# Three edits at the start of a gated attention and MLP kernel: z in rows of four tokens, one accumulator copy on VectorE, scores from the fifth value pair

## The chip, the cores and the metric

The kernel runs on one core of one Trainium2 chip. Its engines are TensorE (PE; PEld is its weight load), VectorE (DVE), ScalarE (ACT), GpSimd (POOL) and SyncE (SP), each with a queue of its own that runs in order. The metric is device time in microseconds (us) of one execution, as the median of several runs.

## The reference

```python
scores = (1/S) * z @ z.T            # per batch: S = 3008 tokens, 64 features
attn   = maximum(scores, 0) ** 2    # S x S
x      = u * (attn @ v)             # S x 256
h      = x @ w_in                   # 256 -> 2048
out    = (h * cos(h)) @ w_out       # 2048 -> 256
```

There are 8 batches; inputs and output are float32. `attn` is symmetric, since both sides of the score are z. The kernel computes in 16-bit floats with 32-bit accumulators.

## The kernel before, in words

The tokens of a batch are cut into 24 rows (k) of 128 and 6 columns (J) of 512. A slot s is one column of one batch; batch 0 has slots 0 to 5. For a slot, `phase_a` or `phase_a_first` multiplies the squared scores of the column with v for all 24 rows, which gives the attention output, transposed, in two halves dh of 128 features. `phase_b` then runs the two matrix products of the hidden layer for earlier slots. No scheduler moves anything: `manual_schedule` keeps each engine's instructions in the order in which the Python code issues them.

**Scores.** `emit_score` makes one score group: two matmuls on half of the array each (L194) into one of the two-bank tiles E, a ReLU by ScalarE into r (L204), and a square by VectorE into a piece A (L209 or L212). A group holds two of the four rows of a block I against column J (h = 0 or 1). Groups come in a fixed order: batch, column J, block I, h. Pieces under the diagonal are later turned by DMA transposes on SP's queue rather than computed.

**Values.** `emit_value` issues the matmuls with v (L258). A row k gives a pair for each dh: the upper 64 tokens go to one accumulator bank, the lower 64 to another, and the two run side by side on the two halves of the array. So a half dh has two banks to add up: one dh uses the two M banks, the other the two banks of an E tile. A step is one such pair.

**The first columns.** Slots 0, 1 and 2 go through `phase_a_first`, in which scores of the next column are made between the steps. With `run` = 2 (slots 1 and 2), steps 0 to 7 are rows 0 to 7 of dh 0, 8 to 15 the same rows of dh 1, 16 to 23 rows 8 to 15 of dh 0, and so on up to step 45; step 46 is the last half row for both. `lo, hi` and `n` say behind which steps the n scores stand (12, 12 and 14 in the three slots): score i stands behind step `lo + (hi - lo) * i // (n - 1)`. In slots 1 and 2 the two gate multiplications of the slot before (`gate_mul`, L286) are issued at step 15, ahead of a score at that step. Score groups that a slot makes itself are needed by it from step 16 on: the first two groups hold rows 8 to 11, the next two rows 12 to 15.

**The end of a column.** `gate_sum` adds up the two banks of one dh: ScalarE copies the first bank to SBUF (L269), VectorE adds the second bank to the copy (L270). This runs for dh 0 and then for dh 1. Until then the banks can't be written again. An E tile goes back to the list `e_order` and the next scores take it. `hold` lets GpSimd read one element of the first sum, so that the load of u behind it starts then. Behind slot 1 stand two units of the hidden layer of slot 0 (`emit_h`: eight matmuls L404, a cosine by ScalarE L412, a product by VectorE L415), and behind slot 2 stands `phase_b(2)` with further units and output matmuls (L525) into the M banks.

**The start.** z of batch 0 comes in six loads of 512 tokens (L633; the last one, of 448, in pieces), issued by SP and ScalarE in turn. The groups are cast to 16 bit (L645; the first three by VectorE, the rest by GpSimd), turned by TensorE against an identity (L649), and copied from PSUM to the tile zT (`copy_turned`: group 0 by ScalarE, L657, the others by VectorE, L659). Seven matmuls on zeros (L664) stand ahead of the first turn, four more (L687) between the first scores.

Of the kernel before, what the change touches and what calls it, by code (L numbers as in the profile page):

```python
# [14 lines left out]
def kernel(  # L15
# [9 lines left out]
    nc = tc.nc  # L25
# [6 lines left out]
    P = 128  # L32
    H = P // 2
    CW = 512
    NB = (S + P - 1) // P
    NC = (S + CW - 1) // CW
# [10 lines left out]
    def width(J):  # L47
        return CW if J < NC - 1 else WL
# [27 lines left out]
    turned = [ppool.tile([P, CW], FP16, name=f"turned{i}", tag=f"M{i % 2}") for i in range(3)]  # L76
# [17 lines left out]
    def drop_piece(key):  # L94
        i = pieces.pop(key)
        if pending.get(i):
            pending[i] = "dropped"
        else:
            free_pieces.append(i)
# [9 lines left out]
    z16s, zTs, vs, u16s, uTs, xs, gs = {}, {}, {}, {}, {}, {}, {}  # L109
# [48 lines left out]
    def turn_u(s):  # L158
        t = upool.tile([P, 8, P], FP16, name="uT")
        nc.sync.dma_start_transpose(t, u16s.pop(s).rearrange("p j d -> p (j d)"))  # L160
        uTs[s] = t
# [20 lines left out]
    def emit_score(later=None):  # L182
        b, J, I, h = groups[done_groups[0]]
        done_groups[0] += 1
        cut = I == J and not (b == 0 and J < 3)
        W = 2 * P if cut and h == 0 else width(J)
        zT = zTs[b]
        e = E[take_e()]
        for t in range(2):
            k = 4 * I + 2 * h + t  # L190
            half = t if h == 0 else 1 - t
            rows = slice(half * H, (half + 1) * H)
            Wt = min(W, (2 * h + t + 1) * P) if cut else W
            nc.tensor.matmul(  # L194
                e[:, t, 0:Wt],
                zT[rows, k * P:(k + 1) * P],
                zT[rows, J * CW:J * CW + Wt],
                start=True,
                stop=True,
            )  # L200
        key = (b, J, I)
        a = new_piece(key) if h == 0 else piece(key)
        r = rpool.tile([P, 2, CW], FP16, name="r")
        nc.scalar.activation(r[:, :, 0:W], e[:, :, 0:W], AF.Relu)  # L204
        def square():
            if I > J:
                a4 = a.rearrange("p (k t j) -> p t k j", k=4, j=P)[:, 2 * h:2 * h + 2, :, :]
                r4 = r.rearrange("p t (k j) -> p t k j", j=P)
                nc.vector.tensor_tensor(a4, r4, r4, ALU.mult)  # L209
            else:  # L210
                a4 = a.rearrange("p (k w) -> p k w", w=CW)[:, 2 * h:2 * h + 2, 0:W]
                nc.vector.tensor_tensor(a4, r[:, :, 0:W], r[:, :, 0:W], ALU.mult)  # L212

        if later is None:
            square()
        else:
            later.append(square)
        if h == 0:
            return
        if cut or (I > J and (b, J, I) not in direct):  # L220
            turns.append(((b, I), key))
            turns.sort(key=lambda t: t[0])
            turn_slots[key] = pieces[key]
            pending[pieces[key]] = "held"

    def emit_turns(due, more=0):
        while turns and (turns[0][0] <= due or more > 0):
            if turns[0][0] > due:
                more -= 1
            (b, c), key = turns.pop(0)  # L230
            b, J, I = key
            i = turn_slots[key]
            a = piece_bufs[i]
            if I == J:
                a4 = a.rearrange("p (k w) -> p k w", w=CW)
                for rr in range(1, 4):
                    rows = P if J * 4 + rr < NB - 1 else H
                    nc.sync.dma_start_transpose(
                        a4[:, 0:rr, rr * P:rr * P + rows],
                        a[0:rows, rr * CW:rr * CW + rr * P],  # L240
                    )
            else:
                d = new_piece((b, I, J))
                nc.sync.dma_start_transpose(d.rearrange("p (n j) -> p n j", j=P), a)
            if pending.pop(i) == "dropped":
                free_pieces.append(i)
# [10 lines left out]
    def emit_value(b, J, k, t, dh, bank, start, stop):  # L257
        nc.tensor.matmul(  # L258
            bank[:, 0:width(J)],
            vs[b, k // 4][t * H:(t + 1) * H, k % 4, dh * P:(dh + 1) * P],  # L260
            value_rhs(b, J, k, t),
            start=start,
            stop=stop,
        )

    def gate_sum(s, b0, b1):
        W = width(s % NC)
        sm = spool.tile([P, CW], FP32, name="sm")
        nc.scalar.copy(sm[:, 0:W], b0[:, 0:W])  # L269
        nc.vector.tensor_tensor(sm[:, 0:W], b1[:, 0:W], sm[:, 0:W], ALU.add)  # L270
        return sm

    def gate_mul(s, dh, sm, eng=None):
        eng = eng or nc.vector
        J = s % NC
        b = s // NC
        W = width(J)
        if s not in xs:
            if J == NC - 1 and b % 2 == 1:
                xs[s] = xodd  # L280
            else:
                xs[s] = xpool.tile([P, 2, CW], FP16, name="x")
        x = xs[s]
        uT = uTs[s].rearrange("p (k d) j -> p k d j", d=2)
        nk = W // P
        eng.tensor_tensor(  # L286
            x[:, dh, 0:nk * P].rearrange("p (k j) -> p k j", j=P),
            sm[:, 0:nk * P].rearrange("p (k j) -> p k j", j=P),
            uT[:, 0:nk, dh, :],
            ALU.mult,  # L290
        )
        if nk < 4:
            dst = x[:, dh, nk * P:W] if b % 2 == 1 else xodd[:, dh, W:CW]
            eng.tensor_tensor(
                dst, sm[:, nk * P:W], uT[:, nk, dh, 0:W - nk * P], ALU.mult
            )
# [44 lines left out]
    late_sums = []  # L341
    mix_at = {9: ("s2", 0), 19: ("s2", 1), 29: ("s4", 0), 35: ("s4", 1)}

    def hold(src):
        nc.gpsimd.tensor_copy(mark[:, 0:1], src)

    def phase_a_first(s, n, extra={}):
        b, J = s // NC, s % NC
        ea = e_order.pop(0)
        pair = [E[ea][:, 0, :], E[ea][:, 1, :]]  # L350
        acc = [pair, M] if s == 1 else [M, pair]
        last = NB - 1
        run = 1 if s == 0 else 2
        steps = [
            (dh, k)
            for I in range(0, NC, run)
            for dh in range(2)
            for k in range(4 * I, min(4 * (I + run), last))
        ] + [(2, last)]
        lo, hi = 5 if s == 0 else 2, 42  # L360
        at = {}
        for i in range(n):
            p = lo + (hi - lo) * i // (n - 1)
            at[p] = at.get(p, 0) + 1
        for i, (dh, k) in enumerate(steps):
            if i in extra:
                extra[i]()
            if dh == 2:
                emit_value(b, J, last, 0, 0, acc[0][0], False, True)
                emit_value(b, J, last, 1, 1, acc[1][1], False, True)  # L370
            else:
                for t in range(2):
                    emit_value(
                        b, J, k, t, dh, acc[dh][t], k == 0, k == last - 1 and t != dh
                    )
            if dh > 0 and (k % 4 == 3):
                drop_piece((b, J, k // 4))
                if s > 0:
                    emit_turns((0, 0), 1)
                    if k < 4:  # L380
                        turn_u(s)
                    elif k < 8:
                        for d in range(2):
                            gate_mul(s - 1, d, late_sums.pop(0))
            for _ in range(at.get(i, 0)):
                emit_score(later=squares if s == 0 and i == lo else None)
        if s == 0:
            turn_u(0)
        late_sums.extend(gate_sum(s, *acc[dh]) for dh in range(2))
        hold(late_sums[0][0:1, 0:1])  # L390
        load_u(s + 1)
        e_order.append(ea)
# [237 lines left out]
    for g in range(NC):  # L630
        eng = nc.sync if g % 2 == 0 else nc.scalar
        full = 4 if g < NC - 1 else 3
        eng.dma_start(  # L633
            z32[g][:, 0:full, :],
            z[0, g * CW:g * CW + full * P, :].rearrange("(j p) d -> p j d", p=P),
        )
        if full == 3:
            for r in range(2):
                nc.sync.dma_start(z32[g][r * H:(r + 1) * H, 3, :], z[0, S - H:S, :])
# [12 lines left out]
            )  # L652

    def copy_turned(g):
        dst = zTs[0][:, g * CW:(g + 1) * CW]
        if g == 0:
            nc.scalar.copy(dst, turned[g])  # L657
        else:
            nc.vector.tensor_copy(dst, turned[g])  # L659

    wc = cpool.tile([P, 2, CW], FP16, name="c")
    nc.scalar.activation(wc[:, 0, 0:P], warm[:, 0:P], AF.Sin)
# [118 lines left out]
```

## Time and profile before

| what | value |
|---|---|
| median of 9 runs | 1193.79 us (1192.93 to 1194.86) |
| the profiled execution | 1192.97 us |
| its span, first to last instruction | 1191.2 us |
| granted TensorE clock, mean | 0.999 |
| TensorE busy | 1183.3 us (99%) |
| VectorE, ScalarE, GpSimd busy | 1011.9, 794.9, 689.5 us |

"L270" is line 270 of the kernel. A row of the timeline has the start, the time from the start of its first to the end of its last instruction, engine, line and operation, what is written and read with its shape, the count, and in brackets how long the engine was idle before and which work ended that. A row of the stretches has length, busy time and count per engine, the granted clock, and the DMA share and rate. Rows of the waits have the total, the number and the longest. Matmuls overlap: the time of one has its tail in it, so the spacing of starts tells the rate.

### The profile page before, as it was taken

The page shows a single profiled execution, that of the slowest core. Times are in us where ns is not written, and L with a number is a line of the kernel's source. Part 1 is how long each engine was busy: PE and PEld are TensorE (multiplying, and loading weights), DVE is VectorE, ACT ScalarE, POOL GpSimd, SP SyncE. Part 2 cuts the span into 40 slices and gives each one's busy share as a digit, 9 for nine tenths or more (in the row PEclk, how much of TensorE's full clock was granted, in tenths as well). Part 3 has the DMA queues.
Part 4 walks back from the last instruction along what each step waited for, and adds up shares of the span by engine and source line. Part 5 has one row for each costly group of instructions (what it writes and reads, how often), then busy time and mean ns, then how long its engine had stood idle before and what let it go on. Part 6 is the DMA issues. An engine that isn't in the chain of part 4 may idle for free. (4 is left out here: it accounts for less than half of the span.)

```text
span 1191.2 us, 29044 instructions
## 1 busy us (share of the span) xinstructions
PE 1183.3 (99%) x11887; PEld 726.3 (61%) x11887; DVE 1011.9 (85%) x1302; ACT 794.9 (67%) x927; POOL 689.5 (58%) x717
## 2 busy tenths in 40 slices
PE   9999999999999999999999999999999999999998
PEld 4556665665566656666566665656666566665566
DVE  6888888889988898888988889888888888888776
ACT  7966676667666676667676676666666666676454
POOL 3286746657466573755647556476565665545452
PEclk9999999999999999999999999999999999999999
DMA  9999998569995699945999559973798838954401
GB/s 160 174 176 154 140 144 131 102 122 132 145 127 101 123 141 160 129 89 103 159 147 133 85 105 162 170 118 70 123 174 138 122 73 126 181 107 84 65 20 54
DMA packets 479862, 148.00 MB, mean 124 GB/s; under 512 B 404208, under 2 KB 479472, under 8 KB 479728
## 3 DMA queue, kind: packets, MB, share of 16 engines
q1 hardware_dynamic: 380752, 112.93, 54.7%
q0 software_dynamic: 97440, 32.78, 27.1%
q8 instruction: 93, 1.52, 0.5%
q10 hardware_dynamic: 1536, 0.43, 0.2%
q14 instruction: 41, 0.34, 0.1%
HBM read 66.32 MB, written 24.64 MB: 76 GB/s over the span
## 5 line engine op out<-in xcount | busy, mean ns | idle before, releaser
L412 ACT ACTIVATE c<-E 128x1024 f16<-128x1024 f32 (+1 forms) x384 | 385.7, 1007 | 216.3 <-PE E L404 214.1
L415 DVE SCALAR_TENSOR_TENSOR g<-E,c 128x1024 f16<-128x1024 f32 (+1 forms) x384 | 458.7, 1196 | 61.7 <-ACT c L412 60.6
L204 ACT ACTIVATE r<-E 128x512 f16<-128x512 f32 (+1 forms) x342 | 327.9, 967 | 112.0 <-PE E L194 106.5
L258 PEld LDWEIGHTS <-v 64*128 64x128 f16 x4512 | 245.2, 94 | 230.0 <-issue 17.9
L404 PE MATMUL E<-x,w_in 128*128 128x512 f16 (+1 forms) x1408 | 354.0, 375 | 0.0
L433 POOL TENSOR_TENSOR s<-g 128x512 f16<-128x512 f16 (+1 forms) x184 | 207.9, 1130 | 189.2 <-DVE g L415 139.4
L258 PE MATMUL M<-A,v 64*128 64x512 f16 (+1 forms) x2256 | 283.0, 372 | 0.0
L258 PE MATMUL E<-A,v 64*128 64x512 f16 (+1 forms) x2256 | 278.0, 372 | 0.0
L434 POOL TENSOR_TENSOR g<-g 128x512 f16<-128x512 f16 (+1 forms) x184 | 219.0, 1190 | 14.4
L404 PEld LDWEIGHTS <-w_in 128*128 128x128 f16 x1536 | 133.1, 98 | 108.9 <-issue 19.5
L482 PEld LDWEIGHTS <-g 128*128 128x128 f16 x2816 | 172.5, 98 | 40.8
L209 DVE TENSOR_TENSOR A<-r 128x1024 f16<-128x1024 f16 x240 | 173.2, 733 | 15.1 <-ACT r L204 14.3
L286 POOL TENSOR_TENSOR x<-sm,uT 128x512 f16<-128x512 f32 (+1 forms) x43 | 48.6, 1130 | 213.4 <-DVE sm L270 213.0
L482 PEld LDWEIGHTS <-s 128*128 128x128 f16 x2112 | 129.4, 98 | 32.0 <-DVE s L440 0.5
L194 PE MATMUL E<-zT 64*128 64x512 f16 (+4 forms) x684 | 127.5, 355 | 1.8 <-DVE sm L270 0.7
L440 DVE TENSOR_TENSOR s<-s,g 128x1024 f16<-128x1024 f16 (+1 forms) x92 | 99.7, 1085 | 2.1 <-POOL s L433 2.1
L482 PE MATMUL M<-w_mix,s 128*128 128x128 f16 x1408 | 94.0, 219 | 0.3 <-POOL s L433 0.3
L482 PE MATMUL M<-w_mix,g 128*128 128x128 f16 x1408 | 93.6, 219 | 0.0
L482 PE MATMUL M<-w_out,g 128*128 128x128 f16 x1408 | 93.6, 219 | 0.0
L212 DVE TENSOR_TENSOR A<-r 128x512 f16<-128x512 f16 (+1 forms) x102 | 80.5, 789 | 8.7 <-ACT r L204 7.9
L194 PEld LDWEIGHTS <-zT 64*128 64x128 f16 x684 | 38.7, 94 | 38.6 <-issue 4.0
L442 DVE TENSOR_TENSOR s<-g,s 128x1024 f16<-128x1024 f16 (+1 forms) x92 | 60.6, 661 | 0.0
(58 smaller groups left out, 647.3 us busy)
## 6 DMA issues: line engine op xcount, KB each, us to landing
out_dram<-o SPq DMA_DIRECT2D x87, 256.0 KB, 2.2
v<-in_v_dram POOLq DMA_DIRECT2D x40, 256.0 KB, 9.0
u<-in_u_dram POOLq DMA_DIRECT2D x40, 256.0 KB, 5.0
A<-A SPq DMA_TRANSPOSE x252, 5.1
z<-in_z_dram POOLq DMA_DIRECT2D x14, 192.0 KB, 10.2
z<-in_z_dram POOLq DMA_DIRECT2D x14, 176.0 KB, 6.1
v<-in_v_dram POOLq DMA_DIRECT2D x8, 192.0 KB, 12.7
u<-in_u_dram POOLq DMA_DIRECT2D x8, 192.0 KB, 3.9
```

What stands on the lines that cost most here:

```text
L194: nc.tensor.matmul(e[:, t, 0:Wt], zT[rows, k * P:(k + 1) * P], zT[rows, J * CW:J * CW + Wt], start=True, stop=True,)
L204: nc.scalar.activation(r[:, :, 0:W], e[:, :, 0:W], AF.Relu)
L209: nc.vector.tensor_tensor(a4, r4, r4, ALU.mult)
L212: nc.vector.tensor_tensor(a4, r[:, :, 0:W], r[:, :, 0:W], ALU.mult)
L258: nc.tensor.matmul(bank[:, 0:width(J)], vs[b, k // 4][t * H:(t + 1) * H, k % 4, dh * P:(dh + 1) * P], value_rhs(b, J, k, t), start=start, ...
L404: nc.tensor.matmul(e[:, f, 0:W], w_in16[:, k, ft * P:(ft + 1) * P], x[:, k, 0:W], start=(k == 0), stop=(k == 1),)
L412: nc.scalar.activation(c[:, :, 0:W], e[:, :, 0:W], AF.Sin, bias=half_pi, scale=inv_s2)
L415: return lambda: nc.vector.scalar_tensor_tensor(gs[m][:, 2 * i:2 * i + 2, 0:W], e[:, :, 0:W], 1.0, c[:, :, 0:W], ALU.mult, ALU.mult)
L433: nc.gpsimd.tensor_tensor(s1[:, f, 0:n], g[:, f, low], g[:, lower, low], ALU.add)
L434: nc.gpsimd.tensor_tensor(g[:, f, low], g[:, f, up], g[:, f, low], ALU.subtract)
L440: nc.vector.tensor_tensor(s2[:, f, 0:n], s1[:, f, 0:n], g[:, f, up], ALU.subtract)
L482: nc.tensor.matmul(acc[:, k * P:(k + 1) * P], left[:, ft, k * P:(k + 1) * P], right[:, ft, :], start=(ft == 0 and k == 0), stop=(ft == F - ...
```

## The change

z loads: in groups 0 to 4, partition p now receives tokens 4p to 4p + 3 of the group, which are 1024 consecutive bytes, where it received tokens p, 128 + p, 256 + p and 384 + p in four runs of 256 bytes. The turned group then has its tokens in another order, and `copy_turned` writes them to zT with a stride of four elements, so that zT is as before. Group 5 stays as it was. The copy of the first bank for dh 0 goes to VectorE in slots 0 to 2; the one for dh 1 stays on ScalarE. In slots 1 and 2 the first score moves from behind step 2 to behind step 5, and the others are spread from there to step 42.

```diff
-    def gate_sum(s, b0, b1):
+    def gate_sum(s, b0, b1, by=None):
         W = width(s % NC)
         sm = spool.tile([P, CW], FP32, name="sm")
-        nc.scalar.copy(sm[:, 0:W], b0[:, 0:W])
+        (by or nc.scalar.copy)(sm[:, 0:W], b0[:, 0:W])
         nc.vector.tensor_tensor(sm[:, 0:W], b1[:, 0:W], sm[:, 0:W], ALU.add)
...
-        lo, hi = 5 if s == 0 else 2, 42
+        lo, hi = 5, 42
...
-        late_sums.extend(gate_sum(s, *acc[dh]) for dh in range(2))
+        late_sums.extend(
+            gate_sum(s, *acc[dh], by=(nc.vector.tensor_copy, nc.scalar.copy)[dh]) for dh in range(2)
+        )
...
-            z[0, g * CW:g * CW + full * P, :].rearrange("(j p) d -> p j d", p=P),
+            z[0, g * CW:g * CW + full * P, :].rearrange(
+                "(p j) d -> p j d" if full == 4 else "(j p) d -> p j d", p=P
+            ),
...
     def copy_turned(g):
-        dst = zTs[0][:, g * CW:(g + 1) * CW]
+        dst, src = zTs[0][:, g * CW:(g + 1) * CW], turned[g]
+        if g < NC - 1:
+            dst = dst.rearrange("q (p j) -> q j p", j=4)
+            src = src.rearrange("q (j p) -> q j p", j=4)
         if g == 0:
-            nc.scalar.copy(dst, turned[g])
+            nc.scalar.copy(dst, src)
         else:
-            nc.vector.tensor_copy(dst, turned[g])
+            nc.vector.tensor_copy(dst, src)
```

## The prediction

> **What bounds the kernel now.** I read the page first, then the busy time of each engine by stretch, then who TensorE waited for, then the order of time on VectorE and TensorE around the ends of the first two columns. The page says that TensorE is the bound:
>
> ```profile
> span 1191.2 us, 29044 instructions
> PE 1183.3 (99%) x11887; PEld 726.3 (61%) x11887; DVE 1011.9 (85%) x1302; ACT 794.9 (67%) x927; POOL 689.5 (58%) x717
> ```
>
> So the span is TensorE's work plus its few idle moments: whatever stops TensorE once is added to the end, and whatever fills a stop is taken off. The change touches the first 55 us only. By stretch (the first number is the length, then PE, PEld, DVE, ACT and POOL busy, PEclk, DMA):
>
> ```profile
> 12.00:24.50 12.50, 12.22 (x112) 6.27 (x112) 8.99 (x14) 12.10 (x14) 2.73 (x5) 1.00 1.25 186
> 24.50:36.00 11.50, 11.12 (x104) 5.72 (x103) 8.75 (x14) 10.76 (x12) 0.79 (x1) 1.00 0.99 174
> 36.00:54.00 18.00, 17.46 (x141) 9.20 (x138) 14.97 (x23) 17.07 (x22) 2.08 (x3) 1.00 1.28 177
> 54.00:100.00 46.00, 46.00 (x401) 28.45 (x401) 41.00 (x44) 30.95 (x36) 40.89 (x38) 1.00 1.26 169
> ```
>
> Columns 0, 1 and 2 fill the first three rows. ScalarE is nearly as full there as TensorE, and TensorE shows only 1.2 us idle in 42: that is the whole prize behind step 12 us. Its waits by name between 12 and 60 us:
>
> ```profile
> PE E L194 <- DVE sm L270: 0.7, 1, 0.7
> PE E L194 <- DVE g L415: 0.4, 1, 0.4
> PE E L194 <- DVE zT L659: 0.2, 1, 0.2
> ```
>
> The first is the end of column 0. Both sums must leave VectorE before a score may write the old accumulator bank:
>
> ```profile
> 22.94 0.69 DVE L212 TENSOR_TENSOR A<-r 128x1024 f16<-128x1024 f16 x1 [0.34 <-ACT r L204]
> 23.55 0.68 DVE L270 TENSOR_TENSOR sm<-M,sm 128x512 f32<-128x512 f32 x1
> 24.15 0.68 DVE L270 TENSOR_TENSOR sm<-E,sm 128x512 f32<-128x512 f32 x1
> ```
>
> ```profile
> 24.88 0.39 PE L194 MATMUL E<-zT 64*128 64x512 f16 x2 [0.66 <-DVE sm L270]
> ```
>
> A matmul's 0.39 includes its tail; starts are 0.2155 apart for a pair of half-array matmuls (six pairs from 22.53, one score among them), so the true stop before 24.88 is 0.84. The end of column 1 has the same shape, with two hidden-layer units of slot 0 behind it:
>
> ```profile
> 37.12 0.68 DVE L270 TENSOR_TENSOR sm<-E,sm 128x512 f32<-128x512 f32 x1
> 37.72 0.68 DVE L270 TENSOR_TENSOR sm<-M,sm 128x512 f32<-128x512 f32 x1
> 38.41 2.35 DVE L415 SCALAR_TENSOR_TENSOR g<-E,c 128x1024 f16<-128x1024 f32 x2
> ```
>
> ```profile
> 38.05 1.21 PE L258 MATMUL M<-A,v 64*128 64x512 f16 x6
> 39.69 0.39 PE L194 MATMUL E<-zT 64*128 64x512 f16 x2 [0.43 <-DVE g L415]
> 40.82 0.39 PE L194 MATMUL E<-zT 64*128 64x512 f16 x2
> ```
>
> By starts, TensorE loses 0.30 before the values in M (38.05 to 38.46), 0.59 before 39.69 and 0.27 before 40.82.
>
> **Part 1, rows of four tokens.** Five loads go from 512 pieces of 256 B to 128 of 1024 B; they may land sooner. The first one gates this:
>
> ```profile
> 3.72 0.82 DVE L645 CAST z<-z 128x512 f16<-128x512 f32 x2 [2.59 <-DMA z<-in_z_dram]
> ```
>
> But TensorE's seven warm-up matmuls start 0.427 apart from 1.19 on and hold it until 4.15, and the first transposition starts at 4.21: a z that is there at once gains 0.06. Later groups are cast well before TensorE asks for them. So 0 to -0.06; I take 0, because the copies behind it get worse: five (one on ScalarE, four on VectorE) now write with a stride of four. ScalarE's stands in the chain to the first score (0.59; its price could rise); VectorE's took 0.42 each. Were they to cost the 0.68 of L270, +0.26 each: the squares behind them wait for ScalarE anyway, and only the fourth copy (10.34) holds a transposition, which starts at 11.05 and would start at 11.07: +0.02, left out of the sum. [...]
>
> **Part 2, one copy on VectorE.** ScalarE loses 0.58 per column, which it does not use: at each column's end the sums wait in VectorE's queue behind the last square, and ScalarE's copies are ready by then. VectorE gains a copy ahead of both adds (the changed program's order: square, copy, add, add). Its price is not in the trace: between 0.42 (L659, 16-bit from PSUM) and 0.68 (L270, 32-bit from PSUM, the nearest). Adds follow each other at 0.60 (23.55, 24.15), so I take 0.60 of queue time; 0.34 would be the low end. Both adds, and what waits for them, are 0.60 later.
>
> **Part 3, scores from step 5.** Step counts of column 1: scores stood at 2, 5, 9, 12, 16 ... and now stand at 5, 8, 11, 15, 18, 21 ...; column 2: 2, 5, 8, 11 ... becomes 5, 7, 10, 13, 16 ... . What the two do together, in time order:
>
> End of column 0: the second add ends at 25.43, the second score starts at 25.48 instead of 24.88, and three more pairs (0.65) are done by then. Net **-0.05**: the later start of the scores only pays for the copy.
>
> Inside column 1, a new wait. The two gate multiplications of slot 0 are issued at step 15, ahead of the score of that step. The fourth score (rows 14 and 15) stood at step 12, so its square ran before them; now it stands at step 15 and its square is queued behind them, as the changed program's order shows (three squares, L286 twice, the fourth square). Before:
>
> ```profile
> 27.46 0.69 DVE L209 TENSOR_TENSOR A<-r 128x1024 f16<-128x1024 f16 x1 [0.39 <-ACT r L204]
> 28.37 0.69 DVE L209 TENSOR_TENSOR A<-r 128x1024 f16<-128x1024 f16 x1 [0.22 <-ACT r L204]
> 28.98 1.28 DVE L286 TENSOR_TENSOR x<-sm,uT 128x512 f16<-128x512 f32 x2
> ```
>
> Its values are used at step 22 (row 14). From the second score's start t: TensorE issues 18 pairs (14 steps, scores two to five and the sixth among them) and wants step 22 at t + 3.88. VectorE: a ReLU starts 0.43 after its score, ReLUs follow at 0.92, a square starts 1.055 after its ReLU: the third square at t + 0.43 + 0.92 + 1.055 = t + 2.41; gates at 3.01 and 3.61; the fourth square at 4.21, ending at 4.90; TensorE goes on at 4.95 (0.05 from an end to a matmul, as 24.83 to 24.88). **+1.07**.
>
> End of column 1: VectorE's order is square, copy, add, add, and two hidden-layer products (1.14 apart). The second add releases M's second bank 0.60 later: at T + 2.93 where it was T + 2.33, T being TensorE's end of the column. Six pairs later the first score finds its buffer free; the second, two steps on, is ready at T + 4.87 and its buffer at T + 5.30. TensorE then has lost 1.65 since T, against 1.48: **+0.18**.
>
> Column 2: 14 scores in 37 steps are 0.83 apart where ReLUs need 0.93 and two buffers circulate. Before they were 0.88 apart and TensorE lost 0.28 late in the column. Walking the scores one by one, the eighth, ninth and tenth wait 0.27, 0.07 and 0.18: **+0.23**; the half-wide ninth lets ScalarE catch up.
>
> End of column 2: the last ReLU is 0.33 later against TensorE than before; then square, copy, add. M's first bank is free at T + 2.06, where the output matmuls are due at T + 1.83: 0.23; the second at T + 2.66 against 2.27: 0.39. **+0.62**. Everything behind has slack (the third unit is due at T + 3.33, its bank free at 3.22).
>
> Sum: -0.05 + 1.07 + 0.18 + 0.23 + 0.62 = +2.05; with the copy at 0.68 of queue time 2.37, at 0.34 about 1.3. I take 2.2, in the upper half, as 0.68 is the nearest row. From 54 us on nothing absorbs it: TensorE has no idle in the 54 to 100 row. The profiled execution took 1192.97 (span 1191.2 and 1.8 around it) and would take 1195.2; the median of the runs is 0.8 above it, so 1196.0.
>
> **Rivals.** (a) Gaps closed, not slower: ScalarE, free of one copy, makes both sums ready early, so the three more pairs cover the stops: 0.84 + 0.30 + 0.59 + 0.27 go, -2.0: 1191.8. For it: ScalarE is 12.1 of 12.5 busy. It decides only if the copy costs VectorE's queue about nothing, and both adds stand behind it there. (b) No wait at step 22, because the square is ready sooner than I count: the sum without 1.07 is +1.0 to 1.3: 1195.0. It needs the square 1.07 sooner, nearly the two gates' 1.20. (c) ScalarE paces column 2: every score waits the 0.10 that it comes too early, 13 x 0.10 = 1.3 in place of 0.23 + 0.28, and the end of the column is later by as much: +3.3: 1197.1; the two buffers' slack at the column's start speaks against it. (d) Part 1 does nothing: my value already.
>
> **How the numbers follow.** Forecast case 0.64, (a) 0.07, (b) 0.11, (c) 0.18. A change under 0.2% (2.4 us) is about what a measurement of this kernel cannot tell from none. The forecast case (1.3 to 3.1, some half of it over 2.4, since waits that I do not see can only add) gives slower 0.32, (c) 0.18: 0.50. Faster by over 0.2% would take all of (a) and more: 0.05. The rest is 0.45. The range from 1193.7 to 1198.4 leaves out (a) and the upper end of (c).
>
> **What would show it.** In the profile after: a VectorE copy of some 0.6 between the last square and the first add; the second score at 25.5; a TensorE stop of about 1 us near 29.4 named after a square (L209), with two L286 just before it; the first values in M 0.6 later behind the hidden units; output matmuls near 56 waiting for VectorE. I am wrong if the copy takes no queue time, if no stop stands near 29.4, or if the first value matmul leaves 8.56 by more than 0.1.

## The result, and the profile after

The changed kernel takes 1197.49 us (median of 9 runs, 1196.63 to 1198.51) where the kernel before took 1193.24 beside it (29 runs): +4.25, a ratio of 1.0033 with a 95% interval of 1.0025 to 1.0042. It is slower, as forecast, and inside the range, but by twice the +2.2 of the sum. The profiled execution took 1196.63, of which the span is 1194.9. The page after, first its span, then the engines:

```profile
span 1194.9 us, 29046 instructions
PE 1183.9 (99%) x11887; PEld 726.4 (61%) x11887; DVE 1016.4 (85%) x1305; ACT 793.9 (66%) x924; POOL 689.5 (58%) x717
```

TensorE's work has not grown (+0.6); the span has, by 3.7. The time is in stops, and TensorE's waits between 4 and 62 us name them (the six largest; total, number, longest):

```profile
PE turned_e L653 <- DVE zT L666: 1.3, 2, 0.8
PE E L194 <- ACT zT L664: 1.2, 1, 1.2
PE E L258 <- DVE A L209: 0.9, 1, 0.9
PE M L258 <- DVE sm L270: 0.8, 1, 0.8
PE E L194 <- DVE sm L270: 0.2, 1, 0.2
PE M L527 <- DMA w_out<-in_moe_w_out_dram: 0.2, 1, 0.2
...
```

The third line is the wait inside column 1 that the prediction named; the fourth and fifth are column ends. The first two were not in the sum at all: they are the copies of turned z, L664 on ScalarE and L666 on VectorE, and together they are the largest item. Those copies in the view by line (duration ns min/median/max, first and last start, shapes):

```profile
L664 ACT COPY zT<-turned x1: 1293/1293/1293, 4.6 to 4.6; 128x512 f16<-128x512 f16 x1
L666 DVE COPY zT<-turned_e x3: 425/1285/1293, 9.3 to 13.3; 128x512 f16<-128x512 f16 x3
L666 DVE COPY zT<-turned x2: 1303/1304/1304, 4.8 to 6.9; 128x512 f16<-128x512 f16 x2
```

All five copies that write with a stride of four elements take 1.28 to 1.30 us, on either engine. The one of 425 ns is group 5, which is written as before. Before, VectorE's took 0.42 and ScalarE's 0.59:

```profile
L659 DVE COPY zT<-turned x2: 424/424/425, 5.3 to 6.5; 128x512 f16<-128x512 f16 x2
L657 ACT COPY zT<-turned x1: 587/587/587, 4.9 to 4.9; 128x512 f16<-128x512 f16 x1
```

TensorE's timeline at the start, up to the first values of column 1, before and then after:

```profile
5.49 0.61 PE L194 MATMUL E<-zT 64*128 64x512 f16 x4 [0.25 <-ACT zT L657]
8.56 1.04 PE L258 MATMUL M<-A,v 64*128 64x512 f16 x8
11.05 0.40 PE L649 MATMUL turned_e<-id,z 128*128 128x128 f16 x4
...
22.53 0.83 PE L258 MATMUL E<-A,v 64*128 64x512 f16 x6
```

```profile
4.15 0.64 PE L653 MATMUL turned<-id,z 128*128 128x128 f16 x8
5.95 0.61 PE L194 MATMUL E<-zT 64*128 64x512 f16 x4 [1.16 <-ACT zT L664]
9.02 1.04 PE L258 MATMUL M<-A,v 64*128 64x512 f16 x8
10.60 0.38 PE L653 MATMUL turned_e<-id,z 128*128 128x128 f16 x4 [0.55 <-DVE zT L666]
12.92 0.38 PE L653 MATMUL turned_e<-id,z 128*128 128x128 f16 x4 [0.75 <-DVE zT L666]
...
24.39 1.47 PE L258 MATMUL E<-A,v 64*128 64x512 f16 x12
```

The first transposition starts 0.06 sooner (4.21 before). The first score starts 0.46 later (5.49), the first values 0.46 (8.56), the transposition of group 4 1.07 later (9.53) and that of group 5 1.87 later (11.05). Column 1's first values stand at 24.39 for 22.53: **+1.86** for the new rows.

Next the end of column 0 and the gates of column 1, on VectorE and on TensorE:

```profile
24.80 0.69 DVE L212 TENSOR_TENSOR A<-r 128x1024 f16<-128x1024 f16 x1 [0.33 <-ACT r L204]
25.41 0.69 DVE L269 COPY sm<-M 128x512 f32<-128x512 f32 x1
26.13 0.69 DVE L270 TENSOR_TENSOR sm<-M,sm 128x512 f32<-128x512 f32 x1
26.74 0.68 DVE L270 TENSOR_TENSOR sm<-E,sm 128x512 f32<-128x512 f32 x1
...
29.87 0.69 DVE L209 TENSOR_TENSOR A<-r 128x1024 f16<-128x1024 f16 x1 [0.22 <-ACT r L204]
30.48 1.28 DVE L286 TENSOR_TENSOR x<-sm,uT 128x512 f16<-128x512 f32 x2
31.68 1.89 DVE L209 TENSOR_TENSOR A<-r 128x1024 f16<-128x1024 f16 x3
```

```profile
27.47 0.39 PE L194 MATMUL E<-zT 64*128 64x512 f16 x2 [0.23 <-DVE sm L270]
...
31.14 0.40 PE L194 MATMUL E<-zT 64*128 64x512 f16 x2
32.42 0.61 PE L258 MATMUL E<-A,v 64*128 64x512 f16 x4 [0.89 <-DVE A L209]
```

VectorE's order is the predicted one. The copy's queue time is 25.41 to 26.13 = 0.72. The fourth square runs behind the two gates, from 31.68 to about 32.37; TensorE issues the score at 31.14, could go on 0.2155 later, and goes on at 32.42: a stop of 1.07. At the end of column 2, VectorE and then TensorE:

```profile
57.23 0.68 DVE L269 COPY sm<-M 128x512 f32<-128x512 f32 x1
57.95 0.69 DVE L270 TENSOR_TENSOR sm<-M,sm 128x512 f32<-128x512 f32 x1
```

```profile
58.21 1.30 PE L527 MATMUL M<-w_out,g 128*128 128x256 f16 x8 [0.20 <-DMA w_out<-in_moe_w_out_dram]
```

The first output matmuls are 0.36 late, by starts, and go on to M's second bank only at 58.69, just behind the add that ends at 58.64. The name in the bracket is new: it is the load of the output weights, not VectorE.

### The profile page after: what moved, and what is told of

The parts are those of the page before. It is cut to its first block, busy times and chain, and to the rows that moved or that the text cites. A ratio compares the mean times of both kernels' runs of the same rounds, so it can differ in the third digit from the quotient of the medians.

```text
span 1194.9 us, 29046 instructions
## 1 busy us (share of the span) xinstructions
PE 1183.9 (99%) x11887; PEld 726.4 (61%) x11887; DVE 1016.4 (85%) x1305; ACT 793.9 (66%) x924; POOL 689.5 (58%) x717
## 3 DMA queue, kind: packets, MB, share of 16 engines
q1 hardware_dynamic: 379600, 112.93, 54.4%
## 4 chain that ended last, share of the span: by engine, by line
PE 95%; ACT 2%; DVE 1%; issue 1%; DMA 0%; POOL 0%; ACTq 0%; DVEq 0%
PE E L406 27%; PE M L484 23%; PE M L258 19%; PE E L258 19%; PE E L194 5%; ACT r L204 1%; PE M L527 1%; PE M L462 1%; DMA A<-A 0%; DVE zT L666 0%; DVE g L417 0%; PE E L671 0%; DVE sm L270 0%; DVE A L212 0%; DVE A L209 0%
## 5 line engine op out<-in xcount | busy, mean ns | idle before, releaser
L436 POOL TENSOR_TENSOR g<-g 128x512 f16<-128x512 f16 (+1 forms) x184 | 219.0, 1190 | 14.4
```

What stands on the lines that cost most here:

```text
L436: nc.gpsimd.tensor_tensor(g[:, f, low], g[:, f, up], g[:, f, low], ALU.subtract)
```

## The experiments

The theory, after the result, is that the strided copies cost what the sum lacks, some 2 us, and that the rest of the sum holds. Against it stand two others: that the copy on VectorE and the later scores cost more than was counted, and that the time is lost at the start by something else than the copies, such as the loads or the clock. The kernel before, run beside the others, took 1193.42 (beside the first four), 1193.33 (the next four) and 1193.77 (the last four). Differences are between medians. Parts are those of the prediction.

**Part 1 taken out.** Loads and copies of z as before, all else as changed:

```diff
-            z[...].rearrange("(p j) d -> p j d" if full == 4 else "(j p) d -> p j d", p=P),
+            z[...].rearrange("(j p) d -> p j d", p=P),
...
-            dst = dst.rearrange("q (p j) -> q j p", j=4)
-            src = src.rearrange("q (j p) -> q j p", j=4)
```

> The change without its first part: z loads and zT copies as before, the copy on VectorE and the scores from step 5 stay. Theory A (the strided zT copies of 1.29 us cost the first 24 us 1.86 us, and the rest of the loss, 2.2, belongs to the copy and the score places): +2.2 us over before, the stop of 1.07 at step 22 of column 1 still there, second column starting at 22.5 as before. Theory B (the loss at the start comes from the two other parts too, for instance through VectorE's queue): less than half of the 1.86 comes back, +3.2 or more.

Measured: 1195.87, +2.45, ratio 1.0018 (1.0009 to 1.0026). The stop inside column 1 is there again, 1.07 before 30.78. So parts 2 and 3 alone cost about what the prediction gave to the whole change (2.2). One thing in this execution had no place in the sum; the view of the tile w_out, its load and then who waited:

```profile
L714 POOL DMA_DIRECT2D w_out<-in_moe_w_out_dram x1: 1162/1162/1162, 41.3 to 41.3; - x1
...
  PE M L527: 1.5, 1
DMA to landing us min/median/max: 16.5/16.5/16.5
```

The weights land at 57.8 and the first output matmuls, whose banks were free, wait for them: 1.66 are lost at the end of column 2, where the sum has 0.62. So the 2.45 is no clean test of the sum's 2.05. Before, the load was issued at 39.1 and landed 14.4 later, 0.9 ahead of its first use at 54.4.

**Part 1 alone.** The same two pieces put into the kernel before:

```diff
-            z[...].rearrange("(j p) d -> p j d", p=P),
+            z[...].rearrange("(p j) d -> p j d" if full == 4 else "(j p) d -> p j d", p=P),
...
+            dst = dst.rearrange("q (p j) -> q j p", j=4)
+            src = src.rearrange("q (j p) -> q j p", j=4)
```

> Before with the first part alone: z in rows of four tokens, zT copies with a stride of four. Theory A: +1.86 us over before, copies of 1.29 on both engines, and the second column starts at 24.4. Theory B: under +0.9.

Measured: 1195.74, +2.32, 1.0020 (1.0011 to 1.0029). The rows alone cost as much as all the rest; the two parts, 2.45 and 2.32, add up to 4.77 against 4.25 for both. In its profile a late full clock stands beside the stop at the copy:

```profile
6.17 1.03 PE L194 MATMUL E<-zT 64*128 64x512 f16 x4 [0.96 <-ACT zT L662]
...
9.50 0.61 PE L692 MATMUL M<-s 128*128 128x512 f16 x1
...
10.57 0.39 PE L692 MATMUL M<-s 128*128 128x512 f16 x1
```

The same matmul takes 0.61 at 9.50 and 0.39 at 10.57: full speed came at 10.51 in this execution, where it came at 5.15 before and at 4.19 in the changed kernel. Column 1 started 2.71 later here, for an expected 1.86; that the stop made the clock late is not shown.

**New loads, plain copies.** Of Part 1 only the loads; the reorder in `copy_turned` is left out, so that the tokens of a group stand in another order in zT. The work is the same.

```diff
-            z[...].rearrange("(j p) d -> p j d", p=P),
+            z[...].rearrange("(p j) d -> p j d" if full == 4 else "(j p) d -> p j d", p=P),
```

> Before with the loads in rows of four tokens, but the zT copies plain as before, so that the tokens of a group stand in another order in zT (the reorder is left out). Theory A (the loads are harmless and the stride is the cost): 0 to -0.1 us, copies of 0.42 and 0.59, the first turn at 4.15 in place of 4.21. Rival (the loads disturb the loads of v or the casts on GpSimd): +0.5 or more with plain copies.

Measured: 1193.70, +0.28, 1.0002 (0.9993 to 1.0011). VectorE's copies take 0.42 and ScalarE's 0.59, the first transposition starts at 4.15 and column 1 0.09 later than before. The loads themselves give and cost nothing that can be measured: the cost of Part 1 is its copies. So it is not the loads.

**Copies that write in order and read with a stride.** Part 1 alone, with the reorder on the PSUM side:

```diff
-            dst = dst.rearrange("q (p j) -> q j p", j=4)
-            src = src.rearrange("q (j p) -> q j p", j=4)
+            dst = dst.rearrange("q (p j) -> q p j", j=4)
+            src = src.rearrange("q (j p) -> q p j", j=4)
```

> Before with the first part, but the copies walk zT in order and read PSUM with a stride of 128 elements (256 bytes) where the change reads in order and writes with a stride of four. If the cost sits in writes of two bytes at a stride: copies between 0.42 and 0.7 us and under +0.3 us. If any stride in such a copy costs the same: copies of about 1.3 us and +1.9 us. If strided reads of PSUM are dearer still: over 1.3 us and more than +2.

Measured: 1194.12, +0.70, 1.0003 (0.9991 to 1.0015). The copies by line, VectorE's of the first groups and ScalarE's:

```profile
L664 DVE COPY zT<-turned x2: 692/692/692, 5.3 to 7.0; 128x512 f16<-128x512 f16 x2
L662 ACT COPY zT<-turned x1: 586/586/586, 4.8 to 4.8; 128x512 f16<-128x512 f16 x1
```

The same data in the same final order: 0.69 in place of 1.30 on VectorE, and ScalarE at its old 0.59. So the price is in the stride of the writing; the stride of the reading took 0.27 on VectorE (0.42 when plain) and nothing on ScalarE. 0.69 is the upper bound that the prediction had taken (0.68), and at it the medians can't tell the cost of the rows from nothing. The profile doesn't bear out the prediction's 0.02 at that price: column 1 starts 0.73 later than before, 0.31 of it ahead of the first values (full clock came at 6.82) and 0.42 behind them.

**Part 2 alone.** The copy on VectorE, scores and z as before:

```diff
-        late_sums.extend(gate_sum(s, *acc[dh]) for dh in range(2))
+        late_sums.extend(
+            gate_sum(s, *acc[dh], by=(nc.vector.tensor_copy, nc.scalar.copy)[dh]) for dh in range(2)
+        )
```

> Before with the second part alone: VectorE makes the dh 0 copy in slots 0 to 2. The copy takes 0.72 of VectorE's queue in the changed kernel (25.41 to 26.13). Theory A (both adds are 0.72 later and TensorE waits for them each time): +0.7 at the end of column 0, +0.7 at the end of column 1, +0.4 at the end of column 2, +1.8 us in all, and no stop at step 22. Rival (ScalarE, free of a copy, gives the time back through earlier ReLUs): 0 to +0.5.

Measured: 1195.07, +1.74, 1.0014 (1.0005 to 1.0023). End of column 0, VectorE and then TensorE:

```profile
23.74 0.69 DVE L269 COPY sm<-M 128x512 f32<-128x512 f32 x1
24.46 0.69 DVE L270 TENSOR_TENSOR sm<-M,sm 128x512 f32<-128x512 f32 x1
25.07 0.68 DVE L270 TENSOR_TENSOR sm<-E,sm 128x512 f32<-128x512 f32 x1
```

```profile
25.80 0.39 PE L194 MATMUL E<-zT 64*128 64x512 f16 x2 [1.39 <-DVE sm L270]
```

The stop before the second score is 1.57 by starts, for 0.84 before: +0.73, the copy's queue time (0.72). The three stops at the end of column 1 grow from 1.06 in all to 1.68, and the output weights are waited for here too, 0.84. No stop stands inside column 1. Nothing hides this copy.

**Part 3 alone.** Scores from step 5, all else as before:

```diff
-        lo, hi = 5 if s == 0 else 2, 42
+        lo, hi = 5, 42
```

> Before with the third part alone: scores from step 5 in slots 1 and 2. Theory A: -0.65 at the end of column 0 (three more pairs in the stop of 0.84), +1.07 at step 22 (fourth square behind the gate multiplications), -0.43 at the end of column 1 and +0.2 in column 2: +0.2 us in all. Rival (the score places make the loss by pacing ScalarE in column 2, whatever the gates): +1 or more, with the loss behind step 41 us.

Measured: 1193.65, +0.32, 1.0001 (0.9992 to 1.0010). By starts: the stop at the end of column 0 falls from 0.84 to 0.20, those of column 1's end from 1.06 in all to 0.64, and the stop inside column 1 is 1.07 as with the whole change. So the later scores do close the gaps, by 1.06 in all, and the wait for the fourth square takes just that back.

**Gates behind the score.** Part 3 alone, with the two gate multiplications issued behind the score of step 15, so that the fourth square runs ahead of them:

```diff
-                    elif k < 8:
-                        for d in range(2):
-                            gate_mul(s - 1, d, late_sums.pop(0))
             for _ in range(at.get(i, 0)):
                 emit_score(later=squares if s == 0 and i == lo else None)
+            if s > 0 and dh == 1 and k == 7:
+                for d in range(2):
+                    gate_mul(s - 1, d, late_sums.pop(0))
```

> Before with scores from step 5, and the two gate multiplications of step 15 issued behind that step's score. Theory A: the fourth square runs ahead of them again, the stop of 1.07 at step 22 is gone and the rest stays: -0.9 us against before, 1.1 less than with the third part alone. Rival (the stop comes from ReLUs that are late, not from the gates): a stop of about 1 us stays near step 22, +0.2.

Measured: 1192.42, -0.91, 0.9997 (0.9987 to 1.0006): 1.23 less than without the move, though not told from before. VectorE, then TensorE:

```profile
28.46 0.69 DVE L209 TENSOR_TENSOR A<-r 128x1024 f16<-128x1024 f16 x1 [0.34 <-ACT r L204]
29.07 1.29 DVE L286 TENSOR_TENSOR x<-sm,uT 128x512 f16<-128x512 f32 x2
```

```profile
29.20 0.61 PE L258 MATMUL E<-A,v 64*128 64x512 f16 x4
```

The square now waits for its ReLU and not for the gates, and TensorE goes on as it ends (29.15). The stop is 0.30, not zero: from score to values there are only seven steps, nine pairs with the scores between them, which take 1.94 at 0.2155, and score, ReLU and square need 2.23 by the spacings in the prediction (0.43 + 1.055 + 0.69 + 0.05).

**The same move in the changed kernel with the old rows.** Parts 2 and 3, with the gates behind the score:

```diff
-                    elif k < 8:
-                        ... gate_mul(s - 1, d, late_sums.pop(0))
...
+            if s > 0 and dh == 1 and k == 7:
+                ... gate_mul(s - 1, d, late_sums.pop(0))
```

> The change without its first part, gate multiplications of step 15 behind that step's score. Theory A: the stop at step 22 goes and nothing else: +1.1 us over before, 1.07 less than the change without its first part. Rival: the time moves into another wait of column 1 or 2, +2.0 or more.

Measured: 1194.47, +1.14, 1.0006 (0.9997 to 1.0016), 1.31 less than the version with the gates in front. The stop falls from 1.07 to 0.29, which is 0.78 of it; the rest is not settled (w_out was waited for 1.66 in the one profile and 0.95 in the other).

**The load of the output weights moved ahead.** It stood behind `phase_a_first(1, 12)`, in GpSimd's queue behind the `hold` on column 1's first sum, so that a later sum starts it later (at 39.1 before, at 43.0 in the changed kernel). Moved ahead of column 1 in the kernel before:

```diff
+    nc.gpsimd.dma_start(w_out16, ...)
     phase_a_first(1, 12)
-    nc.gpsimd.dma_start(w_out16, ...)
```

> Before with the load of w_out (1 MB) issued ahead of column 1 instead of behind it, so that it no longer stands behind the read of that column's first sum. In the profile of before w_out landed 0.9 us ahead of its first use; in six of the variants it landed behind it. Theory C (its landing, 14 to 16.5 us from the issue, is a wait of its own in part of the executions): 0 to -0.3 us against before and less spread. Rival (an early 1 MB load delays u and the transposes): +0.3 or more.

Measured: 1193.17, -0.60, 0.9995 (0.9986 to 1.0003). It is issued at 25.9 and lands 10.9 later, 18 us before its use. The median isn't told from that of before, whose profile had 0.9 to spare. But the spread is smaller, as its first theory said: the slowest of the 11 runs took 1193.62, and 16 of the 30 runs of the kernel before beside it took longer, up to 1195.39. So the late load is probably a wait in part of the executions of the kernel before too, though the one profile kept of it has none; medians that lie a few tenths apart hold this wait in unknown shares.

**The same in the changed kernel.** All three parts, and the load ahead:

```diff
+    nc.gpsimd.dma_start(w_out16, ...)
     phase_a_first(1, 12)
-    nc.gpsimd.dma_start(w_out16, ...)
```

> The change with the same early w_out. Its own profile has 1.86 at the start, 0.08 and 1.07 in column 1, 0.20 and 0.21 in column 2 and 0.63 behind it, 4.05 in all, and w_out landing at 58.17 beside sums that end at 58.64. If w_out only hides behind those sums: 0 to -0.3 us against the change (+4.0 over before). If w_out makes the 0.63: -0.6 and more.

Measured: 1197.07, +3.30, 1.0026 (1.0016 to 1.0036); the whole change had +4.25 in its own comparison. The output matmuls no longer wait for the weights, but for VectorE, and lose the same 0.62, now 0.12 ahead of M's first bank and 0.51 ahead of the second. So in the changed kernel the late load stood beside the sums, and in these two executions none of the 0.62 is its own. The +3.30 is the difference from the highest of the medians of before (1193.77).

**The parts that pay.** Rows and copies as before, scores from step 5, gates behind the score, weights early:

```diff
-        lo, hi = 5 if s == 0 else 2, 42
+        lo, hi = 5, 42
...
-                    elif k < 8:
-                        ... gate_mul(s - 1, d, late_sums.pop(0))
...
+            if s > 0 and dh == 1 and k == 7:
+                ... gate_mul(s - 1, d, late_sums.pop(0))
...
+    nc.gpsimd.dma_start(w_out16, ...)
     phase_a_first(1, 12)
-    nc.gpsimd.dma_start(w_out16, ...)
```

> Scores from step 5 with the gate multiplications behind the score of step 15, and the early w_out; z rows and copies as before. Theory: the gains of both, -0.9 and 0 to -0.3, so -0.9 to -1.2 us against before. Rival (no more room, the two gains are the same wait): -0.9 as without the early w_out.

Measured: 1192.23 (1192.05 to 1192.48), -1.54, 0.9986 (0.9977 to 0.9995): faster than both kernels, and 0.94 under the version with the early load alone (1193.17), which ran beside it. TensorE's waits between 4 and 62 us are down to these:

```profile
PE E L194 <- ACT zT L657: 0.3, 1, 0.3
PE E L194 <- DVE g L415: 0.3, 1, 0.3
PE E L194 <- DVE zT L659: 0.2, 1, 0.2
PE E L194 <- ACT r L204: 0.2, 1, 0.2
```

None of the waits that the change lengthened or brought is in the list: no sum, no square, no weights. By starts, 0.20 is left before the second score of column 1, 0.30 inside column 1 and 0.64 at its end.

**Rows of two tokens.** Part 1 alone at half the run: 512 bytes per piece, copies that write with a stride of two.

```diff
-            z32[g][:, 0:full, :],
-            z[...].rearrange("(j p) d -> p j d", p=P),
+            z32[g].rearrange("p (h j) d -> p h j d", j=2),
+            z[...].rearrange("(h p j) d -> p h j d", p=P, j=2),
...
+            dst = dst.rearrange("q (h p j) -> q h j p", h=2, j=2)
+            src = src.rearrange("q (h j p) -> q h j p", h=2, j=2)
```

> The first part with rows of two tokens (512 bytes): the zT copies write with a stride of two elements (4 bytes) where the change has four (8 bytes). If the cost of 1.29 us comes with any stride: copies of 1.3 and +1.9 us, as with the first part alone. If it depends on how many elements share some short run of SBUF bytes: copies of 0.69 on VectorE (the single rate that reading with a stride showed) and 0.59 on ScalarE, +0.3 to +0.6 us.

Measured: 1194.02, +0.25, 1.0007 (0.9998 to 1.0016). The copies, VectorE's first two and ScalarE's:

```profile
L668 DVE COPY zT<-turned x2: 726/734/743, 5.2 to 6.9; 128x512 f16<-128x512 f16 x2
L666 ACT COPY zT<-turned x1: 729/729/729, 4.8 to 4.8; 128x512 f16<-128x512 f16 x1
```

Stride two costs ScalarE 0.14 and VectorE 0.31 over the plain copy, stride four 0.71 and 0.87. That is near the second case of the expectation, which had ScalarE's copy at its old 0.59.

## Why the prediction was right, and where it was wrong

The terms, in one execution of each kernel (predicted, measured): end of column 0 -0.05, +0.08; inside column 1 +1.07, +1.07; end of column 1 +0.18, +0.20; column 2 +0.23, +0.21; end of column 2 +0.62, +0.63. These sum to 2.05 and 2.19, and the version without Part 1 took 2.45 more than the kernel before, with a longer wait for the weights in it. Part 1 was put at 0 and measured +1.86. 2.19 + 1.86 = 4.05, which is how much later the last hidden-layer product runs; the medians differ by 4.25. The span is longer by 3.7 only, since the last output work of this execution took some 0.4 less; why is open. That 1197.49 lies inside the range is in part luck: the forecast case ended at +3.1, and the room above it was there for rival (c), which did not come.

**The step that failed is the bound on the copies of Part 1.** They were bounded by 0.42 below and 0.68 above; they took 1.29. The upper bound came from a 32-bit operation of the same size, which says what an operation of that size costs when it writes in order, not what a strided write costs. The sentence before it, that ScalarE's copy "stands in the chain to the first score (0.59; its price could rise)", named the right place and gave it no number. With 1.29 the prediction's own walk would have found the rest: ScalarE's copy is 0.70 longer, and VectorE's queue longer still. Third copy to fourth: before, the third starts at 8.51 and the fourth ends at 10.76; after, 9.26 and 12.86. Starting 0.75 later, holding the queue 0.76 longer, 0.27 less for the squares, which no longer wait for ScalarE, and 0.86 more for the fourth copy make 2.10; 0.24 of it was slack, and the last transposition is 1.87 later.

The 1.86 is that of one execution, in two pieces. From the first values to column 1 TensorE took 13.97 in each of the nine profiled kernels with plain copies, 15.38 in the changed kernel and 15.37 in the changed kernel with the early load: 1.40 that is the copies'. (With the rows alone it was 14.35, but there the first values stood 2.33 later than before, behind the stop at the copy and with full clock at 10.51.) Ahead of the first values the changed kernel lost 0.46: ScalarE's copy took 0.70 longer and started 0.25 sooner, as full clock came at 4.19 where it came at 5.15 before and the eight first transpositions took 0.64 for 1.03. The warning "if the first value matmul leaves 8.56 by more than 0.1" was met, by 0.46, but it is no sharp test: with plain copies the first values start between 8.45 and 9.11, and full clock between 4.07 and 7.04.

**The copy on VectorE** took 0.72 of its queue where 0.60 was taken and 0.68 was the upper bound. That is the 0.13 by which the end of column 0 missed; at the other ends it is within what was counted.

**End of column 2** is right in its total and only partly in its cause. The first stop, put at 0.23 for the copy, was 0.36 and waited for the output weights; the second, put at 0.39, was 0.25, because the add that it waits for was the same and TensorE came to it later. With the weights early the two stops are 0.12 and 0.51, and the total is the same: the second add sets it. "Everything behind has slack" overlooked that the weights' load starts behind the first sum of column 1: it had 0.9 to spare, and in the changed kernel that sum comes later and starts the load at 43.0 where it started at 39.1. Of the nine other kernels with the load in its old place, seven waited for it in their profiles.

**The rivals.** (a), gaps closed: its mechanism exists, as the scores from step 5 alone show (0.84 to 0.20), but the copy took 0.72 of VectorE's queue and put the time back, as its condition had said. (b), no wait inside column 1: refuted, 1.07 stood there in every version with scores from step 5 and the gates in front. (c), ScalarE paces column 2: refuted, column 2 lost 0.21. (d), Part 1 does nothing: refuted, it is the largest single part. The chance of no change was too high for the same reason: it rested on a Part 1 of zero.

## What to carry to other kernels

When a load is made contiguous by permuting what it brings, something downstream has to permute it back; find that instruction, ask whether it reads or writes with the stride, and put the stride on the side that costs less (here the reading side: 0.69 and 0.59 where the writing side took 1.30 and 1.29). An operation without a row in the trace needs a bound from what is different about it, not from what is slower in general; if it stands in the chain to the first work of the bound engine, its whole excess may be paid (here 0.70 on ScalarE, and the first score 0.46 later behind a copy that started 0.25 sooner). Work moved later in a queue in order has to be checked against everything that it is now behind, and a load that is started by an event has its slack spent by whatever delays the event (here 0.9: the load started 3.9 later and took 0.8 longer, and its first use was due 3.4 later).

## What the runs showed of the hardware

**Strided 16-bit writes.** A copy of 128x512 16-bit elements from PSUM to SBUF:

| write, read | VectorE | ScalarE |
|---|---|---|
| in order, in order | 0.42 | 0.59 |
| in order, stride of 128 elements | 0.68 to 0.69 | 0.59 |
| stride of 2 elements (4 bytes), in order | 0.72 to 0.74 | 0.73 |
| stride of 4 elements (8 bytes), in order | 1.28 to 1.30 | 1.29 |

With strided writes both engines took the same time here: 0.73 at a stride of four bytes, 1.29 at eight. The same data written in order and read with a stride took 0.69 on VectorE and 0.59 on ScalarE. Other strides of writing were not run, and what makes eight bytes dearer than four is not shown.

**The load of the output weights** (1 MB) took 10.9 to 13.0 us from issue to landing where it was issued at 25 to 28 us, and 14.0 to 16.9 where it was issued at 39 to 43. What slows it there was not tried.

**The start of full clock** varies by execution: 4.07 to 7.04 us in thirteen of the fourteen profiled, and 10.51 in the one with rows alone, seen by the spacing of 512-column matmuls, 0.427 before and 0.2155 after; the trace's record of the granted clock starts at 5.15 in the kernel before and at 4.19 in the changed one. The execution with rows alone had its stop at the copy (0.96 before 6.17) ahead of the rise; the changed kernel had the same stop (1.16 before 5.95) behind it. Whether the stop put the clock off was not tested by itself.
